# Four of twelve tiles get their router logits from VectorE, and their routing a step later

## The chip, the core and the metric

The kernel runs on one core of one Trainium2 chip. Its engines work side by side, each through its own queue in order: TensorE (matrix products), VectorE, ScalarE, GpSimd and SyncE (which here only issues DMAs). The time is the device time of one execution in microseconds; lower is better. The profiler's names are PE for TensorE, PEld for its weight loads, DVE for VectorE, ACT for ScalarE, POOL for GpSimd and SP for SyncE.

## What is computed

An attention with local and global keys, then a gated feed-forward block, then a layer of eight experts with one expert per token and a skip score. The change touches the seam between the last two:

```python
x = (silu * val) @ w_out                    # 1536 tokens x 512, end of the second block
skip_score = x @ w_skip                     # moe2: router
do_compute = skip_score > 0
logits = x[do_compute] @ w_gate             # 512 x 8
e_idx = argmax(logits); probs = softmax(logits)
y[e_idx == e] = gate * (relu(x @ w1[e]) @ w2[e])
out = x; out[do_compute] = x + y
```

## The kernel before

All of it is one program whose order is written out by hand; each engine works through its own list in that order and waits on semaphores where another engine's result is missing.

The second matrix product of the feed-forward block (`gemm2`) makes x for 12 tiles of 128 tokens, one tile in each step of `for t in range(11)`, and tile 11 behind the loop. A step is 36 products of 128x512 into one PSUM buffer: 12 blocks k of three products (h and w_out are split into a high and a low part). Three hooks, called behind blocks 1, 5 and 9, put the other work of the step between the products, so it stands in TensorE's queue at those places.

- At a step's start: `ranks(t-2)` (two small matmuls that count the tokens ahead in each expert, into a PSUM buffer), `select(t-2)` and `gates(t-2)` on VectorE (eight small instructions, L707 to L693; they end in `sel` and `val`).
- Hook `one`: `turn(t-1)` transposes x of the tile before on TensorE (L580) and ScalarE copies it to `x2t` (L581); `split_h(t+1)` makes the high and low part of h for the next step on ScalarE and VectorE (six instructions each, L567 and L568).
- Hook `two`: `routed(t-1)`: the logits by four matmuls of TensorE against `w9t` (w_gate and w_skip, 9 columns; each shows as two records in the trace), `route` on VectorE (L653 to L674: maximum, mask `oh`, running count `cum`, negated maximum), and `exps` on ScalarE (L677). Then `split_next`: casts of experts' weights, the high part on ScalarE (L845) and the low part on VectorE (L854), and `load_next`, loads of such weights on SP's queue.
- The third hook: `slots(t-2)`, one matmul that reads `sel` and `val`.

The logits and the ranks take turns in two PSUM buffers of one tag (`ps1`). The experts' raw weights and their casts live in slots: eight of a pool `raw`, and the tiles of h that have been used up. Eight chunks of 128x1024 are loaded ahead of the stage and cast in steps 2 (three), 3 (two), 6 (two) and 7 (one); four more are loaded in step 7 and six in step 10. Behind the stage, the experts take the other chunks as slots come free.

Of the kernel before, what the change touches and what calls it, by code (L numbers as in the profile page):

```python
# [8 lines left out]
F32 = mybir.dt.float32  # L9
# [6 lines left out]
ALU = mybir.AluOpType  # L16
# [11 lines left out]
def f(ap):  # L28
    return ap.bitcast(F32)
# [529 lines left out]
def split_h(s, t):  # L559
    nc = s.nc  # L560
    hh = s.hspool.tile([128, 12, 128], F32R, name="hh", bufs=2)
    hl = s.hspool.tile([128, 12, 128], F32R, name="hl", bufs=2)
    c = slice(128 * (t % 4), 128 * (t % 4) + 128)
    for q in range(6):
        i = slice(2 * q, 2 * q + 2)
        src = s.h[t // 4, q][:, :, c]
        nc.scalar.copy(hh[:, i, :], src)  # L567
        nc.vector.tensor_tensor(hl[:, i, :], src, f(hh[:, i, :]), ALU.subtract)  # L568
    s.hs[t] = hh, hl


def turn(s, t, h=None):

    nc = s.nc
    ks = range(4) if h is None else range(2 * h, 2 * h + 2)
    if not h:
        s.xt[t] = s.hpool.tile([128, 4, 128], F32, name="x2t", bufs=2)
    p = s.ps_n.tile([128, len(ks), 128], F32, name="pxt", tag="rb", bufs=2)
    for k in ks:
        nc.tensor.transpose(p[:, k - ks[0], :], s.x2[t][:, 128 * k:128 * k + 128], s.ident)  # L580
    nc.scalar.copy(s.xt[t][:, ks[0]:ks[-1] + 1, :], p)  # L581
# [7 lines left out]
        s.nc.tensor.matmul(s.lg[t], lhsT=s.xt[t][:, k, :], rhs=s.w9t[:, k, :], start=k == 0, stop=k == 3)  # L589


def gemm2(s, t, hooks={}):

    nc = s.nc
    hh, hl = s.hs.pop(t)
    x2 = s.x2[t] = s.hpool.tile([128, 512], F32, name="x2", bufs=3)

    N = 256 if t == 11 else 512
    for c in range(0, 512, N):
        p = s.ps_g.tile([128, N], F32, name="px", tag="ps0", bufs=2)  # L600
        n = 0
        for k in range(12):
            for h, w in ((hh, s.woh), (hh, s.wol), (hl, s.woh)):
                nc.tensor.matmul(p, lhsT=h[:, k, :], rhs=w[k][:, c:c + N], start=n == 0, stop=n == 35)  # L604
                n += 1
            if (c, k) in hooks:
                hooks[c, k]()
        nc.scalar.activation(x2[:, c:c + N], p, AF.Copy, scale=s.r[t // 6][:, t % 6:t % 6 + 1])
    nc.sync.dma_start(s.xm[128 * t:128 * t + 128, :], x2)
    if t < 11:  # L610
        nc.scalar.dma_start(s.out[128 * t:128 * t + 128, :], x2)
# [36 lines left out]
def route(s, t):  # L648

    V, p = s.nc.vector, s.ixpool if t == 11 else s.hpool  # L650
    lg, skip = s.lg[t][:, 0:8], s.lg[t][:, 8:9]
    m = s.rm[t] = (s.ixpool if t >= 10 else p).tile([128, 1], F32, name="rm", bufs=2)
    V.tensor_reduce(m, lg, AX.X, ALU.max)  # L653
    do = s.do = p.tile([128, 1], F32, name="rdo", bufs=2)
    V.tensor_scalar(do, skip, 0.0, None, ALU.is_gt)
    yield
    c = p.tile([128, 8], F32, name="rc", bufs=2)
    V.scalar_tensor_tensor(out=c, in0=lg, scalar=m, in1=s.m8, op0=ALU.is_equal, op1=ALU.mult)
    yield
    e = p.tile([128, 1], F32, name="re", bufs=2)  # L660
    V.tensor_reduce(e, c, AX.X, ALU.min)
    yield
    V.scalar_tensor_tensor(out=s.oh[:, t, :], in0=c, scalar=e, in1=do.to_broadcast([128, 8]),
                           op0=ALU.is_equal, op1=ALU.mult)
    yield
    V.tensor_scalar(s.val[:, t, 0, :], s.oh[:, t, :], s.tok1[:, t:t + 1], None, ALU.mult)
    V.tensor_tensor(s.cum[:, t + 1, :], s.cum[:, t, :], s.oh[:, t, :], ALU.add)


def exps(s, t):  # L670

    nc, V, p = s.nc, s.nc.vector, s.ixpool if t >= 10 else s.hpool
    m = s.rm[t]
    V.tensor_scalar(m, m, -1.0, None, ALU.mult)  # L674
    z = s.rz[t] = p.tile([128, 1], F32, name="rz", bufs=2)
    ex = p.tile([128, 8], F32, name="rex", bufs=2)
    nc.scalar.activation(ex, s.lg.pop(t)[:, 0:8], AF.Exp, bias=m, accum_out=z)  # L677


def gates(s, t):  # L680

    nc, V, p = s.nc, s.nc.vector, s.ixpool if t >= 10 else s.hpool
    z = s.rz.pop(t)
    V.tensor_scalar(z, z, 1e-9, None, ALU.add)
    yield
    V.reciprocal(z, z)
    yield
    g = p.tile([128, 8], F32, name="rg", bufs=2)
    V.tensor_scalar(g, s.oh[:, t, :], z, None, ALU.mult)
    yield  # L690
    V.tensor_copy(s.val[:, t, 1, :], g)
    yield
    V.tensor_tensor(s.val[:, t, 2, :], g, f(s.val[:, t, 1, :]), ALU.subtract)  # L693


def ranks(s, t, pool=None, tag="ps1"):

    rk = s.rk[t] = (pool or s.ps_g).tile([128, 8], F32, name="rk", tag=tag, bufs=1 if pool else 2)
    s.nc.tensor.matmul(rk, lhsT=s.ones16, rhs=s.cum[:, t, :], start=True, stop=False)
    s.nc.tensor.matmul(rk, lhsT=s.tri, rhs=s.oh[:, t, :], start=False, stop=True)  # L700


def select(s, t):

    V = s.nc.vector
    c = (s.ixpool if t >= 9 else s.hpool).tile([128, 8], F32, name="rp", bufs=2)
    V.tensor_tensor(c, s.oh[:, t, :], s.rk[t], ALU.mult)  # L707
    yield
    V.tensor_reduce(s.pos[:, t:t + 1], c, AX.X, ALU.add)
    yield  # L710
    sel = s.sel[t] = (s.ixpool if t >= 9 else s.hpool).tile([128, 256], F32R, name="sel", bufs=3 if t >= 9 else 2)
    V.tensor_scalar(sel, s.slot, s.pos[:, t:t + 1], None, ALU.is_equal)
    yield


def slots(s, t):

    if t in (0, 9):
        s.sl = s.ps_m.tile([24, 256], F32, name="sl", tag="misc", bufs=1)
    s.nc.tensor.matmul(s.sl, lhsT=s.val[:, t, :, :].rearrange("p a e -> p (a e)"), rhs=s.sel[t],  # L720
                       start=t in (0, 9), stop=t in (8, 11))


def run(*parts):

    parts = list(parts)
    while parts:
        parts = [p for p in parts if next(p, FAR) is None]
# [213 lines left out]
def attn_moe_kernel(ctx, tc, qx, kx, vx, rel, ints, wgv, w_out, rms_g, w9, w9t, w1, w2, out):  # L942
    s = K()
    nc = s.nc = tc.nc
# [4 lines left out]
    def pool(stack, name, side=None, space=None):  # L949
        kw = {} if space is None else {"space": space}  # L950
        return stack.enter_context(
            tc.tile_pool(name=name, bufs=1, side=side, reuse_waits="tile", **kw))
# [165 lines left out]
    rawpool = pool(phase3, "raw", side="right")  # L1118
# [11 lines left out]
        halves += [(j + 1, 0)] * (j < 8) + [(j, 1)]  # L1130
    loads = iter([(j, 4 * half + c) for j, half in halves for c in range(4)])
    s.slots = Slots()
    s.slots.add(rawpool, [f"raw{z}" for z in range(8)])

    def load_next(n, eng=nc.sync):
        for _ in range(n):
            x = next(loads, None)
            if x:
                if x == (8, 0):
                    experts[8].e = nc.values_load(  # L1140
                        s.eji[0:1, 0:1], engines=[mybir.EngineType.SP], min_val=0, max_val=7,
                        skip_runtime_bounds_check_because="a minimum with 7 of a count")
                experts[x[0]].load(x[1], eng)
# [5 lines left out]
    def split_next(n):  # L1149
        for _ in range(n):  # L1150
            x = next(chunks, None)
            if x:
                experts[x[0]].split(x[1], nc.scalar, nc.vector)

    load_next(8)
    s.early = s.ixpool.tile([128, 512], F32, name="early", bufs=1)
    nc.gpsimd.memset(s.early, 0.0)

    def routed(t):
        logits(s, t)  # L1160
        run(route(s, t))
        exps(s, t)

    for t in range(11):
        if t >= 2:
            ranks(s, t - 2)
            run(select(s, t - 2))
        if t >= 2:
            run(gates(s, t - 2))

        def one():
            if t >= 1:
                turn(s, t - 1)
                split_h(s, t + 1)
            if t in (2, 6, 10):
                for q in range(6):
                    s.slots.add(early if t < 10 and q == 0 else big, [f"h{t // 4}{q}"])
                load_next({6: 0, 10: 6}.get(t, 0))

        def two():  # L1180
            if t >= 1:
                routed(t - 1)
            split_next({2: 3, 3: 2, 6: 2, 7: 1}.get(t, 0))
            load_next({7: 4}.get(t, 0))

        gemm2(s, t, {(0, 1): one, (0, 5): two, (0, 9): lambda: t >= 2 and slots(s, t - 2)})


    slt = s.ixpool.tile([24, 256], F32, name="slt", bufs=1)
# [46 lines left out]
    def keep(n):  # L1236

        w = experts[0].w[0][0]
        for _ in range(n):
# [19 lines left out]
                                   op0=ALU.is_equal, op1=ALU.mult)  # L1259
# [82 lines left out]
    with tc.For_i(1, more, 1) as j:  # L1342
        lgi, lsi, lgate = job_slots(s, s.epool, ds(j, 1))
        e = nc.values_load(s.eji[0:1, ds(j, 1)], engines=[mybir.EngineType.SP], min_val=0, max_val=7,
                           skip_runtime_bounds_check_because="a minimum with 7 of a count")
# [85 lines left out]
```

## Time and profile before

| | before |
|---|---|
| median of three runs | 554.51 us (551.69 to 555.45) |
| the profiled execution | 554.08 us, its span 552.3 us |
| TensorE busy | 524.2 us (95%) |
| VectorE busy | 404.8 us (73%) |
| ScalarE busy | 277.5 us (50%) |
| GpSimd busy | 140.8 us (25%) |
| second matrix product, twelve steps | from 303.28 to about 428 us of the span |

The span is the profiled execution from its first to its last instruction. A timeline row gives the start, the length, the engine, the line and the instruction (output <- inputs, shapes); rows that follow each other on an engine may be joined with a count. The length of a row may overlap the next one on the same engine, so the distance of two starts is what a row takes of its queue. A row of busy time by stretch gives the stretch, its length, the busy us and the instructions (x) of TensorE, its weight loads, VectorE, ScalarE and GpSimd, then TensorE's granted clock as a share of full speed, the busy share of the DMA engines and GB/s. In the rows of waits, the engine in front waited for the one behind the arrow.

### The profile page before, as it was taken

The page shows a single profiled execution, that of the slowest core. Times are in us where ns is not written, and L with a number is a line of the kernel's source. Part 1 is how long each engine was busy: PE and PEld are TensorE (multiplying, and loading weights), DVE is VectorE, ACT ScalarE, POOL GpSimd, SP SyncE. Part 2 cuts the span into 40 slices and gives each one's busy share as a digit, 9 for nine tenths or more (in the row PEclk, how much of TensorE's full clock was granted, in tenths as well). Part 3 has the DMA queues.
Part 4 walks back from the last instruction along what each step waited for, and adds up shares of the span by engine and source line. Part 5 has one row for each costly group of instructions (what it writes and reads, how often), then busy time and mean ns, then how long its engine had stood idle before and what let it go on. Part 6 is the DMA issues. An engine that isn't in the chain of part 4 may idle for free. (4 is left out here: it accounts for less than half of the span.)

```text
span 552.3 us, 9096 instructions
## 1 busy us (share of the span) xinstructions
PE 524.2 (95%) x3132; PEld 425.8 (77%) x3132; DVE 404.8 (73%) x1026; ACT 277.5 (50%) x631; POOL 140.8 (25%) x140
## 2 busy tenths in 40 slices
PE   3899886999999999999999999999999999999994
PEld 2676665878888888888888888878789787888883
DVE  5899999567888688868884358456443599999971
ACT  2799896324332233333333255244231587988850
POOL 2446545001222212212220200000000512666001
PEclk9999998999999999999999999999999999999998
DMA  8653511112323323323313512116171599999300
GB/s 301 210 211 139 173 36 39 33 46 77 105 88 113 113 79 114 114 79 113 115 38 130 214 39 78 39 52 215 39 293 57 202 393 395 398 399 396 131 15 16
DMA packets 28997, 80.62 MB, mean 146 GB/s; under 512 B 3512, under 2 KB 3768, under 8 KB 28945
## 3 DMA queue, kind: packets, MB, share of 16 engines
q1 hardware_dynamic: 24400, 68.61, 35.0%
q0 software_dynamic: 2672, 8.22, 3.9%
q10 hardware_dynamic: 1872, 3.15, 1.6%
q8 instruction: 26, 0.43, 0.3%
q14 instruction: 27, 0.21, 0.1%
HBM read 72.28 MB, written 8.65 MB: 147 GB/s over the span
## 5 line engine op out<-in xcount | busy, mean ns | idle before, releaser
L538 PE MATMUL ps<-xh,wh 128*128 128x512 f32 (+1 forms) x304 | 115.4, 380 | 0.1
L538 PE MATMUL ps<-xh,wl 128*128 128x512 f32 (+1 forms) x304 | 115.0, 378 | 0.5 <-POOL wl L504 0.5
L538 PE MATMUL ps<-xl,wh 128*128 128x512 f32 (+1 forms) x304 | 114.9, 378 | 0.0
L854 DVE TENSOR_TENSOR ewl<-eraw,ewh 128x1024 fp32r<-128x1024 f32 x72 | 83.5, 1220 | 6.2 <-ACT ewh L845 5.9
L845 ACT CAST ewh<-eraw 128x1024 fp32r<-128x1024 f32 x72 | 71.3, 1055 | 6.2 <-DVE ewl L854 4.2
L538 PEld LDWEIGHTS ps<-xh,wl 128*128 128x128 f32 x304 | 57.2, 188 | 11.6 <-POOL wl L504 0.9
L491 DVE SCALAR_TENSOR_TENSOR wraw<-f64t,wraw 128x512 f32<-128x512 f32 x36 | 44.7, 1241 | 28.8 <-ACT f64t L489 28.8
L538 PEld LDWEIGHTS ps<-xh,wh 128*128 128x128 f32 x304 | 57.2, 188 | 11.0 <-issue 0.7
L538 PEld LDWEIGHTS ps<-xl,wh 128*128 128x128 f32 x304 | 57.2, 188 | 10.6
L604 PE MATMUL px<-woh,hh 128*128 128x512 f32 (+1 forms) x156 | 61.8, 396 | 0.0
L604 PE MATMUL px<-woh,hl 128*128 128x512 f32 (+1 forms) x156 | 58.7, 376 | 0.0
L604 PE MATMUL px<-wol,hh 128*128 128x512 f32 (+1 forms) x156 | 58.2, 373 | 0.0
L504 POOL TENSOR_TENSOR wl<-f64t,wh 128x512 fp32r<-128x512 f32 x24 | 31.0, 1293 | 101.3 <-ACT wh L503 55.7
L503 ACT CAST wh<-f64t 128x512 fp32r<-128x512 f32 x24 | 14.9, 622 | 71.4 <-DVE f64t L501 68.1
L262 ACT ACTIVATE es<-es,m 128x192 f32<-128x192 f32 (+1 forms) x96 | 41.4, 434 | 11.5 <-DVE m L251 10.3
L278 POOL TENSOR_SCALAR es<-es,z 128x192 f32<-128x192 f32 x46 | 36.0, 791 | 36.2 <-ACT pts L297 11.7
L286 PE MATMUL pt<-ident,es 128*128 128x128 f32 x176 | 30.5, 305 | 10.1 <-DVE pts L295 6.6
L286 PEld LDWEIGHTS pt<-ident,es 128*128 128x128 f32 x176 | 20.7, 152 | 21.6 <-DVE pts L295 10.0
L568 DVE TENSOR_TENSOR hl<-h,hh 128x256 fp32r<-128x256 f32 x72 | 25.4, 422 | 15.8 <-ACT hh L567 15.8
L604 PEld LDWEIGHTS px<-woh,hl 128*128 128x128 f32 x156 | 29.3, 188 | 5.8
L604 PEld LDWEIGHTS px<-woh,hh 128*128 128x128 f32 x156 | 29.4, 188 | 4.9
L604 PEld LDWEIGHTS px<-wol,hh 128*128 128x128 f32 x156 | 29.5, 189 | 4.0
(195 smaller groups left out, 979.7 us busy)
## 6 DMA issues: line engine op xcount, KB each, us to landing
eraw<-in_w_dram SPq DMA_DIRECT2D x64, 512.0 KB, 11.2
wraw<-in_wgv_dram SPq DMA_DIRECT2D x24, 512.0 KB, 3.8
wraw<-in_w_out_dram SPq DMA_DIRECT2D x12, 512.0 KB, 3.5
vp<-in_vx_dram SPq DMA_DIRECT2D x8, 704.0 KB, 4.0
eraw<-in_w_dram POOLq DMA_DIRECT2D x8, 512.0 KB, 13.6
kd<-in_kx_dram SPq DMA_DIRECT2D x7, 464.0 KB
xm<-x SPq DMA_DIRECT2D x12, 256.0 KB
out_dram<-x ACTq DMA_DIRECT2D x12, 256.0 KB, 2.8
```

The costliest lines, as they stand in the source:

```text
L262: nc.scalar.activation(e[:, r, x, e0:e0 + n], e[:, r, x, e0:e0 + n], AF.Exp, bias=m[:, j:j + 1], scale=-1.0, accum_out=z[:, j:j + 1])
L278: eng.tensor_scalar(e[:, r, x, e0:e0 + n], e[:, r, x, e0:e0 + n], z[:, j:j + 1], None, ALU.mult)
L286: nc.tensor.transpose(pt[:, kt, x, :], e[:, r, x, 128 * kt:128 * kt + 128], s.ident)
L491: nc.vector.scalar_tensor_tensor(out=a.bitcast(F32), in0=t, scalar=F64_LEAST, in1=a.bitcast(F32), op0=ALU.is_ge, op1=ALU.mult)
L503: nc.scalar.copy(hi, t)
L504: eng.tensor_tensor(lo, t, f(hi), ALU.subtract)
L538: nc.tensor.matmul(p, lhsT=w[:, k, :], rhs=x[c][:, k, a:b], start=n == 0, stop=n == 11)
L568: nc.vector.tensor_tensor(hl[:, i, :], src, f(hh[:, i, :]), ALU.subtract)
L604: nc.tensor.matmul(p, lhsT=h[:, k, :], rhs=w[k][:, c:c + N], start=n == 0, stop=n == 35)
L845: eng.copy(wh, raw)
L854: eng.tensor_tensor(wl, raw, f(wh), ALU.subtract)
```

## The change

Tiles 1, 3, 5 and 7 (`rows`) no longer get transposes and logits matmuls. `row_logits` takes their logits on VectorE: nine instructions, one for each column of w9, that multiply x of the tile (128x512) by a row of w9 which lies on all 128 partitions and sum the result into one number per token. Five of them stand in the first hook of the step behind the tile, four in the next step's. The routing of such a tile (`route`, `exps`) moves from the second hook of step t+1 to that of step t+2, ahead of the next tile's; its ranks, select and gates (`ranked`) move from the start of step t+2 to its third hook; its slots matmul moves from the third hook of step t+2 to the first hook of step t+3. The other tiles keep their places.

The nine rows of w9 are broadcast by five DMAs on SP's queue into five tiles `w9b`, in the place of five of the eight `raw` slots, which become slots again in step 9. Three chunks instead of eight are loaded ahead of the stage. Casts come two in step 2, one each in 3, 6, 7 and 8, and two in 9; loads come two in step 2, one each in 3, 6, 7 and 8, three in 9 and six in 10.

```diff
--- before.py
+++ after.py
@@ -589,6 +589,16 @@
         s.nc.tensor.matmul(s.lg[t], lhsT=s.xt[t][:, k, :], rhs=s.w9t[:, k, :], start=k == 0, stop=k == 3)
+def row_logits(s, t, es):
+    if es[0] == 0:
+        s.lg[t] = s.hpool.tile([128, 9], F32, name="lgd", bufs=1)
+    for e in es:
+        s.nc.vector.tensor_tensor_reduce(
+            out=s.w9b[4][:, 512:1024], in0=s.x2[t], in1=s.w9b[e // 2][:, 512 * (e % 2):512 * (e % 2) + 512],
+            scale=1.0, scalar=0.0, op0=ALU.mult, op1=ALU.add, accum_out=s.lg[t][:, e:e + 1])
 def gemm2(s, t, hooks={}):
     nc = s.nc
@@ -1130,7 +1140,11 @@
         halves += [(j + 1, 0)] * (j < 8) + [(j, 1)]
     loads = iter([(j, 4 * half + c) for j, half in halves for c in range(4)])
     s.slots = Slots()
-    s.slots.add(rawpool, [f"raw{z}" for z in range(8)])
+    s.slots.add(rawpool, [f"raw{z}" for z in range(3)])
+    s.w9b = [rawpool.tile([128, 1024], F32, name=f"w9b{z}", bufs=1) for z in range(5)]
+    for z in range(5):
+        rows = w9[2 * z:min(2 * z + 2, 9), :].rearrange("(o e) n -> o (e n)", o=1)
+        nc.sync.dma_start(s.w9b[z][:, 0:rows.shape[1]], rows.to_broadcast([128, rows.shape[1]]))
     def load_next(n, eng=nc.sync):
         for _ in range(n):
@@ -1152,7 +1166,7 @@
             if x:
                 experts[x[0]].split(x[1], nc.scalar, nc.vector)
-    load_next(8)
+    load_next(3)
     s.early = s.ixpool.tile([128, 512], F32, name="early", bufs=1)
     nc.gpsimd.memset(s.early, 0.0)
@@ -1161,29 +1175,53 @@
         run(route(s, t))
         exps(s, t)
+    rows = (1, 3, 5, 7)
+    def ranked(t):
+        ranks(s, t)
+        run(select(s, t))
+        run(gates(s, t))
     for t in range(11):
-        if t >= 2:
-            ranks(s, t - 2)
-            run(select(s, t - 2))
-        if t >= 2:
-            run(gates(s, t - 2))
+        if t >= 2 and t - 2 not in rows:
+            ranked(t - 2)
         def one():
+            if t - 3 in rows:
+                slots(s, t - 3)
             if t >= 1:
-                turn(s, t - 1)
+                if t - 1 not in rows:
+                    turn(s, t - 1)
                 split_h(s, t + 1)
+            if t - 1 in rows:
+                row_logits(s, t - 1, range(5))
+            if t - 2 in rows:
+                row_logits(s, t - 2, range(5, 9))
             if t in (2, 6, 10):
                 for q in range(6):
                     s.slots.add(early if t < 10 and q == 0 else big, [f"h{t // 4}{q}"])
-                load_next({6: 0, 10: 6}.get(t, 0))
+            if t == 10:
+                load_next(6)
         def two():
-            if t >= 1:
+            if t - 2 in rows:
+                run(route(s, t - 2))
+                exps(s, t - 2)
+            if t >= 1 and t - 1 not in rows:
                 routed(t - 1)
-            split_next({2: 3, 3: 2, 6: 2, 7: 1}.get(t, 0))
-            load_next({7: 4}.get(t, 0))
-        gemm2(s, t, {(0, 1): one, (0, 5): two, (0, 9): lambda: t >= 2 and slots(s, t - 2)})
+            if t == 9:
+                s.slots.add(rawpool, [f"w9b{z}" for z in range(5)])
+            split_next({2: 2, 3: 1, 6: 1, 7: 1, 8: 1, 9: 2}.get(t, 0))
+            load_next({2: 2, 3: 1, 6: 1, 7: 1, 8: 1, 9: 3}.get(t, 0))
+        def three():
+            if t - 2 in rows:
+                ranked(t - 2)
+            elif t >= 2:
+                slots(s, t - 2)
+        gemm2(s, t, {(0, 1): one, (0, 5): two, (0, 9): three})
     slt = s.ixpool.tile([24, 256], F32, name="slt", bufs=1)
```

What stands in the queues, first on VectorE in the middle of step 3 (`hl` is h's low part for the next step, `x_3564` is tile 1's x, `lgd` its logits; the bare `ISA lgd` reads the sum out). Before:

```order
L568 TENSOR_TENSOR hl<-h_2039,hh 128x256 [waits Activation_49]
L653 TENSOR_REDUCE rm<-lg 128x1 [waits PE_49]
L655 TENSOR_SCALAR rdo<-lg 128x1
L658 SCALAR_TENSOR_TENSOR rc<-lg,rm,m_3485 128x8 [waits DVE_49]
L661 TENSOR_REDUCE re<-rc 128x1 [waits DVE_49]
L663 SCALAR_TENSOR_TENSOR oh<-rc,re,rdo 128x8 [waits DVE_49]
```

Now:

```order
L568 TENSOR_TENSOR hl<-h_2039,hh 128x256 [waits Activation_49]
L597 ISA w9b_3509,lgd<-x_3564,w9b_3507 128x512 [waits DVE_49]
L597 ISA lgd 128x1
L597 ISA w9b_3509,lgd<-x_3564,w9b_3508 128x512 [waits DMAHW5_49,DVE_49]
L597 ISA lgd 128x1
L597 ISA w9b_3509,lgd<-x_3564,w9b_3508 128x512 [waits DVE_49]
L597 ISA lgd 128x1
L597 ISA w9b_3509,lgd<-x_3564,w9b_3509 128x512 [waits DMAHW6_49,DVE_49]
L597 ISA lgd 128x1
L663 TENSOR_REDUCE rm<-lgd 128x1
L665 TENSOR_SCALAR rdo<-lgd 128x1 [waits DVE_49]
L668 SCALAR_TENSOR_TENSOR rc<-lgd,rm,m_3485 128x8 [waits DVE_49]
```

Between the split of h and the first routing now stand four products of the row tile; the first routing is the row tile's (`lgd`), and the routing of the even tile follows it.

Second, ScalarE in step 3, from the last part of h's split (`rex` is the exponential, `ewh` the high part of a weight cast, `x_` the copy of the step's x out of PSUM). Before:

```order
L567 CAST hh<-h_2039 128x256
L677 ACTIVATE rex,rz<-lg,rm 128x8 [waits DVE_49,PE_49]
L845 CAST ewh<-eraw 128x1024 [waits DMAHW5_49]
L845 CAST ewh<-eraw 128x1024
L608 ACTIVATE x_3770<-px,r_1376 128x512 [waits DMAHW3_49,DMAHW0_49,PE_49]
```

Now:

```order
L567 CAST hh<-h_2039 128x256
L687 ACTIVATE rex,rz<-lgd,rm 128x8 [waits DVE_49]
L687 ACTIVATE rex,rz<-lg,rm 128x8 [waits DVE_49,PE_49]
L855 CAST ewh<-eraw 128x1024 [waits DMAHW2_49]
L618 ACTIVATE x_3735<-px,r_1376 128x512 [waits DMAHW3_49,PE_49]
```

There are two exponentials in a row where one stood, and one cast where two stood.

Third, TensorE over the end of step 3 and the start of step 4. Before (from the last product of step 3):

```order
L604 MATMUL px<-woh_2023,hl 128x512
L699 LDWEIGHTS ones_3498
L699 MATMUL rk<-cum,ones_3498 128x8
L700 LDWEIGHTS tri
L700 MATMUL rk<-oh,tri 128x8 [waits DVE_49]
L604 MATMUL px<-woh_2018,hh 128x512 [waits Activation_49]
L604 MATMUL px<-wol_2024,hh 128x512
L604 MATMUL px<-woh_2018,hl 128x512
L604 MATMUL px<-woh_2018,hh 128x512
L604 MATMUL px<-wol_2024,hh 128x512
L604 MATMUL px<-woh_2018,hl 128x512
L580 MATMUL pxt<-ident,x_3770 128x128 [waits Activation_49]
```

Now:

```order
L614 MATMUL px<-woh_2023,hl 128x512
L709 LDWEIGHTS ones_3498
L709 MATMUL rk<-cum,ones_3498 128x8 [waits Activation_49]
L710 LDWEIGHTS tri
L710 MATMUL rk<-oh,tri 128x8 [waits DVE_49]
L614 MATMUL px<-woh_2018,hh 128x512
L614 MATMUL px<-wol_2024,hh 128x512
L614 MATMUL px<-woh_2018,hl 128x512
L614 MATMUL px<-woh_2018,hh 128x512
L614 MATMUL px<-wol_2024,hh 128x512
L614 MATMUL px<-woh_2018,hl 128x512
L730 MATMUL sl<-sel,val 24x256 [waits DVE_49]
```

The ranks at the step's start (tile 2's in both) now wait for ScalarE too, and behind six products the slots matmul of tile 1 stands where a transpose stood.

## Rows read from the trace of the kernel before

**Rows 1.** Busy time in stretches: step 6 from 360.71, last step, experts; counts in brackets.

```profile
360.71:370.61 9.90, 9.90 (x54) 8.04 (x54) 6.28 (x24) 5.36 (x12) 0.00 (x0) 1.00 0.15 55
...
410.20:428.00 17.80, 17.79 (x144) 16.54 (x144) 6.18 (x38) 3.64 (x10) 1.27 (x1) 1.00 0.36 132
...
464.00:500.00 36.00, 36.00 (x172) 29.44 (x171) 36.00 (x39) 32.76 (x41) 21.56 (x6) 1.00 1.04 399
```

**Rows 2.** Waits, steps 2 to 10: who waited for whom, us in total, times, longest.

```profile
DVE rp L707 <- PE rk L700: 19.2, 7, 3.2
```

**Rows 3.** TensorE's timeline, steps 5 and 6: start us, us, line, instruction.

```profile
350.81 0.47 PE L604 MATMUL px<-woh,hh 128*128 128x512 f32 x1
...
352.26 0.60 PE L580 MATMUL pxt<-ident,x 128*128 128x128 f32 x4
...
352.62 0.48 PE L604 MATMUL px<-woh,hh 128*128 128x512 f32 x1
...
352.93 0.40 PE L604 MATMUL px<-wol,hh 128*128 128x512 f32 x1
...
353.16 0.40 PE L604 MATMUL px<-woh,hl 128*128 128x512 f32 x1
...
355.48 0.96 PE L589 MATMUL lg<-w9t,x2t 128*128 128x9 f32 x8
...
356.29 0.47 PE L604 MATMUL px<-woh,hh 128*128 128x512 f32 x1
...
359.13 0.28 PE L720 MATMUL sl<-sel,val 128*24 128x256 f32 x1
...
360.71 0.47 PE L604 MATMUL px<-woh,hh 128*128 128x512 f32 x1
```

**Rows 4.** VectorE's timeline, step 6 (from 360.71).

```profile
363.74 2.10 DVE L568 TENSOR_TENSOR hl<-h,hh 128x256 fp32r<-128x256 f32 x6 [1.15 <-ACT hh L567]
...
366.38 0.17 DVE L653 TENSOR_REDUCE rm<-lg 128x1 f32<-128x8 f32 x1 [0.53 <-PE lg L589]
...
367.04 0.23 DVE L663 SCALAR_TENSOR_TENSOR oh<-rc,re,rdo 128x8 bf16<-128x8 f32 x1
...
367.51 0.15 DVE L674 TENSOR_SCALAR rm<-rm 128x1 f32<-128x1 f32 x1
...
369.09 2.36 DVE L854 TENSOR_TENSOR ewl<-eraw,ewh 128x1024 fp32r<-128x1024 f32 x2 [1.43 <-ACT ewh L845]
...
371.36 0.16 DVE L707 TENSOR_TENSOR rp<-oh,rk 128x8 f32<-128x8 bf16 x1
...
372.87 0.17 DVE L693 TENSOR_TENSOR val<-rg,val 128x8 fp32r<-128x8 f32 x1
```

**Rows 5.** ScalarE's timeline, step 6.

```profile
367.75 0.27 ACT L677 ACTIVATE rex<-lg,rm 128x8 f32<-128x8 f32 x1 [2.51 <-DVE rm L674]
...
368.01 1.99 ACT L845 CAST ewh<-eraw 128x1024 fp32r<-128x1024 f32 x2
```

**Rows 6.** VectorE's instructions by shape: attention's add-and-reduce; busy us, mean ns.

```profile
L251 DVE CUSTOM_DVE_ANT_0 es<-sc,bias 128x192 f32<-128x192 f32 x80 | 25.3, 351 | 1.1 <-PE sc L240 1.1
...
L251 DVE CUSTOM_DVE_ANT_0 es<-sc,bias 128x64 f32<-128x64 f32 x8 | 1.7, 218 | 0.0
```

**Rows 7.** Line 491: duration ns min/median/max; one of its instructions in VectorE's timeline.

```profile
L491 DVE SCALAR_TENSOR_TENSOR wraw<-f64t,wraw x36: 678/1375/1798, 55.4 to 284.1; 128x512 f32<-128x512 f32 x36
...
185.00 0.69 DVE L491 SCALAR_TENSOR_TENSOR wraw<-f64t,wraw 128x512 f32<-128x512 f32 x1 [1.42 <-ACT f64t L489]
```

**Rows 8.** SP's timeline: the experts' loads after the stage.

```profile
432.65 74.05 SPq L837 DMA_DIRECT2D eraw<-in_w_dram  x46
```

**Rows 9.** Busy time in stretches, end of the attention: TensorE and its granted clock.

```profile
88.00:90.00 2.00, 0.40 (x8) 0.16 (x3) 2.00 (x9) 1.30 (x7) 2.00 (x3) 1.00 0.69 256
...
92.00:93.00 1.00, 1.00 (x12) 0.78 (x8) 0.93 (x4) 0.77 (x3) 0.58 (x2) 0.51 0.08 16
...
99.00:100.00 1.00, 1.00 (x8) 0.72 (x5) 0.00 (x0) 0.75 (x2) 0.00 (x0) 1.00 0.00 0
```

## Prediction

> **What bounds the kernel now.** I read the busy time by stretch first, the waits second, and then laid the rows of one step of the second matrix product side by side. That stage runs from about 303 to 428 us of a span of 552.3 us, in twelve steps, one tile of 128 tokens each. A full step takes 9.9 us and TensorE is busy in all of it, while VectorE and ScalarE are busy for five to six of it [rows 1]. In the list of waits of steps 2 to 10 no row has TensorE waiting for an engine: VectorE and ScalarE wait, among them VectorE for the ranks matmul, up to 3.2 us at a time [rows 2]. So a microsecond taken off TensorE's queue there is a microsecond off the time, as long as VectorE still delivers before TensorE comes to what it needs. After the stage, the experts' stage starts from what the stage leaves, and VectorE and the DMA engines are full there [rows 1]. Its loads wait for slots which the stage sets free (46 issues from 432.65 us on [rows 8]). I therefore let every gain or loss of the stage go through to the end unchanged.
>
> The question is thus what VectorE's and ScalarE's rows give to TensorE, and when. Time is counted below from S, the first product of an odd step (3, 5, 7 or 9). All four of them now carry the second part of a row tile, t-2, and the whole routing of two tiles.
>
> **What leaves TensorE.** For four tiles the four transposes and four logits matmuls go. The transposes hold the queue for 0.36 us (352.26 to 352.62) and lengthen the next product by 0.08 (0.31 to the one after, against 0.23). The logits hold it for 0.81 and again 0.08 [rows 3]. That is 1.33 us a tile, 5.3 us in all. Ranks and slots matmuls stay as many as before and only change place: 0 for their own durations. ScalarE loses four copies, which nothing waited for.
>
> **What a product costs on VectorE.** A multiply-and-sum over 128x512 is in no row. The same kind of instruction in the attention takes 218 ns for 64 columns and 351 ns for 192 [rows 6]: 1.04 ns per column, so 684 ns for 512. The listing shows that each waits for the one ahead of it (they share a scratch output). If they overlap like their neighbours the step from one to the next is 0.61 us, with the full wait it is 0.73. I take 0.69: four are 2.8 us, five are 3.5.
>
> [...] First the row: an instruction with two fp32 sources in SBUF and 512 columns (L491) takes between 678 and 1798 ns, with a median of 1375 [rows 7]. So the same form runs both at about 1.04 ns per column and at twice that. In the step of [rows 1] GpSimd is idle, as in its neighbours, and L491 takes 0.69 us at 185.00 [rows 7], where no GpSimd instruction lies beside it, so I count the product at the short end. [...]
>
> **An odd step, laid out.** VectorE's split of h ends at S+5.13 (363.74 plus 2.10, with S at 360.71) [rows 4]. Nothing before it changes: the even tile's transpose and copy stay. Four products bring VectorE to S+7.9. The row tile's routing follows: its mask oh is ready 0.89 us after the routing begins (366.38 to 367.04 plus 0.23), at S+8.8. TensorE comes to the ranks of that tile at the place where the slots matmul stood, at S+8.32 (350.81 to 359.13) [rows 3]. With 0.1 us for a handover between engines (VectorE's rm ended 0.09 us before the exponential began [rows 4, 5]) it waits 0.55 us.
>
> The second tile's routing starts 1.2 us after the first (the rows of one routing) at S+9.1. The exponential ends 1.64 us after a routing begins (366.38 to 367.75 plus 0.27 [rows 4, 5]), at S+10.75. The next ranks matmul writes the PSUM buffer that this exponential reads; before, logits and ranks never shared a buffer, now three of the four such places name ScalarE as releaser in the listing. TensorE would be there at S+9.87 plus 0.55, and waits about 0.45. So an odd step has 1.0 us of new waits, four make 4.0 us, and the even step begins at about S+10.9.
>
> **The even step behind it.** Its second hook puts the row tile's slots matmul after six products, 1.45 us into the step (350.81 to 352.26): TensorE is there at S+12.35. What it waits for stands on VectorE behind the odd step's weight casts. ScalarE's cast begins right after the exponential, 1.63 us after the second routing's start (366.38 to 368.01), at S+10.75; VectorE's half starts 1.08 later (369.09), and takes 1.18 (2.36 for two) [rows 4, 5]. Then come select and gates, 1.68 us from 371.36 to the end of 372.87. That is S+14.7, plus the handover: a wait of 2.4 us. Step 5 has no cast: select begins at S+10.4 and ends before S+12.3, so step 6 does not wait. Steps 3 and 7 have one cast, and steps 4 and 8 wait 2.4 us each. Step 9 has two casts, 1.18 more, and step 10 waits 3.6. Together 8.4 us. Before, select and gates also stood behind the casts, but the slots matmul that needs them came 8.3 us into the step and was never late; the cover was that distance, and it is gone. Behind the waiting slots matmul stands all of TensorE's queue.
>
> **The rest.** Over a pair of steps VectorE has 4.2 us of splits, 6.2 of products, 2.5 of routing, 3.4 of select and gates and up to 3.5 of casts, 19.8 at most, against 19.8 us for the pair before: so its queue never falls behind by more than a step, and the split for the next step, which TensorE needs at its start, stays early. On the SP queue five broadcasts of w9 take the place of five weight loads ahead of the stage, with no more bytes; the first product needs them in step 2, two steps later. The weight loads in steps 2, 3 and 6 to 9 stand two or more steps ahead of their casts, except those of steps 8 and 9, which feed the experts' stage: eighteen chunks are loaded and eight cast by its start, as before. I take 0 for these; if the nine late loads were not done in time, the first experts would wait, but their 4.7 MB take 12 us at the 399 GB/s of [rows 1], and the last step alone has 17.8.
>
> **Sum.** 4.0 + 8.4 - 5.3 = 7.1 us more. The profiled execution took 554.1 us by itself (span 552.3 us and 1.8 around it), against a median of 554.5. So 554.1 + 7.1 = **561.2 us**. With products 0.61 or 0.73 us apart and handovers between 0 and 0.2 us this case lies between 558.5 and 564.
>
> **Rivals.**
> *The waits do not come (faster).* VectorE is idle for a third or more of a step [rows 1], and if its rows came 2.4 us earlier than I laid them, every matmul would find its operands ready. The saving alone gives 554.1 - 5.3 = 548.8. It decides from select and gates ending by S+12.3 in cast steps. Against it: in the odd step nine rows of routing for two tiles, four products and the cast hang on each other in one queue. Chance 0.10.
> *The waits cancel the saving (same).* The short waits in odd steps vanish (products of 0.5 us, or handovers of nothing) and those at the slots shrink by 0.9 us each, to 1.5, 1.5 and 2.7: 5.7 - 5.3, about 554.5, and up to 559 on the way to my case. Chance 0.15.
> *Products at twice the length.* 0.69 us more for each: four in an odd step delay its ranks by 2.8 us, four times 11 us: 572. It needs the long form of [rows 7] without GpSimd. Chance 0.05.
> *The waits lower TensorE's clock.* Before, the granted clock stood at 1.00 in this stage [rows 1], where TensorE never paused. [...] Against it: around each wait the products stand close. Chance 0.15. [...]
>
> **How the numbers follow.** My forecast has 0.55. About 1% (5.5 us) is what a measurement of this kernel can tell from no change. Faster than 548.6 needs the first rival: 0.10. Slower than 559.6 are most of my case (0.45 of 0.55), the clock and the long products: 0.65. The rest is 0.25. From 556 to 571 all is held but the first rival, half of the second and the third, about 0.2.
>
> **What would show it.** In the changed profile, waits of TensorE for VectorE at slots in steps 4, 8 and 10 of some 2.4, 2.4 and 3.6 us and none in 6, and short ones at ranks in odd steps; steps of about 10.9, 11.0, 10.9, 8.5, 10.9, 11.0, 10.9 and 13.5 us from 3 to 10; products of 0.6 to 0.73 us. It is wrong if TensorE has no wait there, if the products take 0.4 or 1.3 us, if the clock falls, or if the experts' stage gets longer or shorter by itself.

## The result, and the profile after

The changed kernel takes 562.45 us (median of four runs, 561.57 to 563.54), the kernel before beside it 553.1 us (551.66 to 555.45). The ratio is 1.0148, with a 95% interval from 1.0127 to 1.0169: slower by about 8.2 us. The four runs of the kernel before lie in two pairs, near 551.7 and near 555 us, with its median between them, so the medians are 9.35 us apart where the ratio says 8.2. The forecast was 561.2 us.

| profiled execution | before | after |
|---|---|---|
| time | 554.08 us | 563.54 us, the longest of its four |
| span | 552.3 us | 561.8 us |
| second matrix product, first to last product's start | 119.50 us | 128.37 us |
| up to that stage | 303.28 us | 303.72 us |
| behind it | 129.5 us | 129.7 us |

So 8.87 of the 9.5 us arise in the stage. Its steps, each from its first product to the next step's first:

| step | 2 | 3 | 4 | 5 | 6 | 7 | 8 | 9 | 10 |
|---|---|---|---|---|---|---|---|---|---|
| before | 9.91 | 9.91 | 9.89 | 9.90 | 9.91 | 9.91 | 9.90 | 9.90 | 9.91 |
| forecast | - | 10.9 | 11.0 | 10.9 | 8.5 | 10.9 | 11.0 | 10.9 | 13.5 |
| after | 8.41 | 10.84 | 12.46 | 10.39 | 8.59 | 10.79 | 10.84 | 10.77 | 14.99 |

Where [rows 2] had no wait of TensorE in these steps, there are ten now. The list of waits of the changed kernel from 320 to 430 us (us in total, times, longest):

```profile
PE sl L730 <- DVE val L703: 7.5, 3, 3.2
PE rk L710 <- DVE oh L673: 1.4, 4, 0.4
PE rk L709 <- ACT rex L687: 1.1, 3, 0.4
```

TensorE's timeline shows them one by one. At 338.65 and 340.68 are the two of step 3, then the slots matmuls of steps 4, 6, 8 and 10; that of step 6 has no wait:

```profile
338.65 0.17 PE L710 MATMUL rk<-oh,tri 128*128 128x8 bf16 x1 [0.39 <-DVE oh L673]
...
340.68 0.17 PE L709 MATMUL rk<-cum,ones 128*128 128x8 bf16 x1 [0.39 <-ACT rex L687]
...
344.47 0.30 PE L730 MATMUL sl<-sel,val 128*24 128x256 f32 x1 [2.11 <-DVE val L703]
...
365.06 0.29 PE L730 MATMUL sl<-sel,val 128*24 128x256 f32 x1
...
386.70 0.30 PE L730 MATMUL sl<-sel,val 128*24 128x256 f32 x1 [2.11 <-DVE val L703]
...
409.45 0.30 PE L730 MATMUL sl<-sel,val 128*24 128x256 f32 x1 [3.24 <-DVE val L703]
```

What VectorE did ahead of step 3's wait for the mask and step 4's for `val`, in step 3 (from 329.89) and the start of step 4; rows between are left out:

```profile
332.88 2.11 DVE L568 TENSOR_TENSOR hl<-h,hh 128x256 fp32r<-128x256 f32 x6 [1.69 <-ACT hh L567]
334.90 0.69 DVE L597 CUSTOM_DVE_ANT_0 w9b<-x,w9b 128x512 f32<-128x512 f32 x1
335.51 0.09 DVE L597 DVE_READ_ACCUMULATOR2_ANT lgd<- 128x1 f32 x1
335.63 0.69 DVE L597 CUSTOM_DVE_ANT_0 w9b<-x,w9b 128x512 f32<-128x512 f32 x1
...
337.72 0.16 DVE L663 TENSOR_REDUCE rm<-lgd 128x1 f32<-128x8 f32 x1
...
338.37 0.23 DVE L673 SCALAR_TENSOR_TENSOR oh<-rc,re,rdo 128x8 bf16<-128x8 f32 x1
...
341.60 1.23 DVE L864 TENSOR_TENSOR ewl<-eraw,ewh 128x1024 fp32r<-128x1024 f32 x1 [1.42 <-ACT ewh L855]
342.75 0.15 DVE L717 TENSOR_TENSOR rp<-oh,rk 128x8 f32<-128x8 bf16 x1
...
344.25 0.17 DVE L703 TENSOR_TENSOR val<-rg,val 128x8 fp32r<-128x8 f32 x1
```

The mask `oh` is done at 338.60, and the ranks matmul runs at 338.65. Select (342.75) begins only when the cast has ended, `val` is done at 344.42, and the slots matmul runs at 344.47: a handover of 0.05 us each time.

The waits are 10.0 us, and the steps 2 to 10 grew by 98.08 - 89.14 = 8.94 us, though TensorE also gave work away. The granted clock tells what else came in. Busy time by stretch (columns as in [rows 1]), steps 4, 6, 8 and 10:

```profile
340.73:353.19 12.46, 10.35 (x40) 7.97 (x40) 9.41 (x33) 3.36 (x8) 0.00 (x0) 0.86 0.26 85
...
363.58:372.17 8.59, 8.59 (x41) 6.83 (x40) 8.07 (x32) 3.98 (x10) 0.00 (x0) 1.00 0.36 123
...
382.96:393.80 10.84, 8.73 (x40) 6.82 (x40) 9.42 (x34) 4.31 (x9) 0.00 (x0) 1.00 0.12 48
...
404.57:419.56 14.99, 11.75 (x54) 9.25 (x54) 8.41 (x32) 5.14 (x12) 0.00 (x0) 0.89 0.76 255
```

Closer, behind the slots matmuls of steps 4, 8 and 10:

```profile
346.00:347.00 1.00, 1.00 (x4) 0.81 (x3) 1.00 (x5) 0.00 (x0) 0.00 (x0) 0.50 0.90 354
...
386.70:388.00 1.30, 1.30 (x7) 1.08 (x8) 1.12 (x7) 1.00 (x2) 0.00 (x0) 1.00 0.00 0
...
410.00:411.00 1.00, 1.00 (x5) 0.81 (x4) 0.85 (x6) 0.65 (x2) 0.00 (x0) 0.50 1.04 402
```

In steps 4 and 10 the granted clock fell to 0.50 after TensorE had resumed; in step 8, behind a wait of the same 2.11 us, it stayed at 1.00. At the low level a product takes 0.42 us of the queue instead of 0.23 (two neighbours in step 4, and in step 8):

```profile
345.50 0.63 PE L614 MATMUL px<-woh,hh 128*128 128x512 f32 x1
345.92 0.63 PE L614 MATMUL px<-wol,hh 128*128 128x512 f32 x1
```

```profile
387.53 0.39 PE L614 MATMUL px<-woh,hh 128*128 128x512 f32 x1
387.76 0.40 PE L614 MATMUL px<-wol,hh 128*128 128x512 f32 x1
```

With step 6 as the even step without a wait, the 8.94 us come apart. The waits are +10.0. The row tiles save 1.50 in step 2 and 1.32 in each of 4, 6 and 8: -5.5. The clock costs 1.6 in step 4 (12.46 - 8.59 - 2.11 - 0.14) and 1.7 in step 10 (14.99 - 9.91 - 3.24 - 0.14): +3.3. The 0.14 is what step 8 is longer beside its listed wait (10.84 - 8.59 - 2.11); three of them, and 0.15 beside the listed waits in each odd step, are +1.0. Sum: 8.8. The 0.15 is not the price of a wait: step 5 of the run with two outputs below has no wait in its list, has the ranks in their new place, and takes 10.03 us, 0.13 more than before.

Behind the stage little changed; the last step and the experts' stretch, which answer to the second and third row of [rows 1]:

```profile
419.56:437.30 17.74, 17.73 (x144) 16.48 (x144) 6.17 (x38) 3.63 (x10) 1.27 (x1) 1.00 0.33 121
...
472.00:508.00 36.00, 36.00 (x175) 29.34 (x174) 36.00 (x39) 31.88 (x40) 20.70 (x6) 1.00 1.04 398
```

### The profile page after: what moved, and what is told of

Read it like the earlier page. It is cut to its first block, busy times and chain, and to the rows that moved or that the text cites. A ratio compares the mean times of both kernels' runs of the same rounds, so it can differ in the third digit from the quotient of the medians.

```text
span 561.8 us, 9084 instructions
## 1 busy us (share of the span) xinstructions
PE 522.9 (93%) x3084; PEld 423.1 (75%) x3084; DVE 428.2 (76%) x1098; ACT 275.6 (49%) x627; POOL 140.3 (25%) x140
```

## Experiments

Each edit is against the changed kernel. Ratios are to the kernel before, which ran on the same chip (medians 554.45 to 554.81 us); "stage" is the first to the last product's start, 119.50 us before and 128.37 after.

### Casts, loads and broadcasts alone

```diff
-    rows = (1, 3, 5, 7)
+    rows = ()
```

> The set of row tiles is empty: all twelve tiles take their logits from TensorE as before, but the five broadcasts of w9 and the new places of casts and loads stay. This takes the moved casts and loads by themselves. Theory (as in the prediction, which counted them at nothing): no difference from the kernel before, within 1 us of it, steps of 9.9 us and no wait of TensorE in the stage. Rival: the broadcasts or the shifted loads cost part of the 9.5 us by which the span of the changed kernel is longer, so 1 to 3 us more than before, seen as a later start of the stage (303.7 instead of 303.3 us), or as an experts' stage that is longer than before.

Measured: 554.66 us, ratio 0.9998 (0.9982 to 1.0013). No step is longer than 9.92 us, there is no wait of TensorE in the stage, and the stage has 119.50 us. It begins at 303.76 us though; in the other runs it begins anywhere from 303.26 to 304.68, in no relation to their edits, so half a microsecond ahead of the stage can't be put down to the change. Moved casts, loads and broadcasts cost nothing by themselves.

### One row tile, at two places

```diff
-    rows = (1, 3, 5, 7)
+    rows = (3,)
```

> Only tile 3 takes its logits from VectorE. Its odd step is step 5, which has no cast, and step 6 is the one whose slots matmul did not wait. Theory (price by place): step 4 is 1.3 us shorter, step 5 about 0.5 longer (the wait for the mask and its restart), step 6 as before: 0.9 us less than before in all, about 1 us under it. Rival (every row tile costs the same share of the 9 us): 2.3 us more than before.

Measured: 553.98 us, ratio 0.9986 (0.9968 to 1.0004). Step 4 has 8.43 us, step 5 has 10.39 with one wait of 0.33, step 6 has 10.03: 28.85 us for the three against 29.70 before, 0.85 less where 0.9 was expected. The stage has 118.24. Its other steps are some 0.05 us shorter each, as are the untouched steps of the next run; no run shows why. The interval of the time includes no change.

```diff
-    rows = (1, 3, 5, 7)
+    rows = (7,)
```

> Only tile 7 takes its logits from VectorE. Its odd step is step 9, with two casts, and its slots matmul stands in step 10, where TensorE waited 3.24 us. Theory (price by place): step 8 is 1.3 us shorter, step 9 about 0.9 longer, step 10 longer by the wait of 3.2 and, if the clock falls behind it as it did, by 1.7 more: 4.6 us more than before, or 3.0 if the clock stays. Rival (every row tile costs the same share): 2.3 us more.

Measured: 558.3 us, ratio 1.0062 (1.0047 to 1.0077), some 3.4 us more. Its waits in TensorE's timeline:

```profile
398.68 0.17 PE L710 MATMUL rk<-oh,tri 128*128 128x8 bf16 x1 [0.33 <-DVE oh L673]
...
400.72 0.17 PE L709 MATMUL rk<-cum,ones 128*128 128x8 bf16 x1 [0.38 <-ACT rex L687]
...
405.64 0.41 PE L730 MATMUL sl<-sel,val 128*24 128x256 f32 x1 [3.24 <-DVE val L703]
```

Steps 8, 9 and 10 have 8.44, 10.78 and 15.02 us, the last with a stretch at half clock. The time lies between the two that were expected, 3.0 us more if the clock stays up and 4.6 if it falls. Its two longest executions (559.76 and 560.13 us, the last the profiled one) have a mean granted clock of 0.985, the three shortest (557.25 to 558.17 us) one of 0.991 or 0.992, so the clock probably did not fall there in every execution.

The same move of work is a small gain in its own steps for tile 3, as expected, and a loss for tile 7. The tiles differ in what stands between the routing and the slots matmul; the runs with moved casts and slots below test that. An equal share of 2.3 us is outside both intervals.

### The waits filled with work

```diff
             if t - 3 in rows:
+                fill({4: 9, 8: 9, 10: 14}.get(t, 0), t)
                 slots(s, t - 3)
```

`fill(n, t)` issues n products of 128x512 into a PSUM tile that nothing reads.

> The changed kernel with idle products of 128x512 into an unused PSUM tile ahead of the slots matmul of a row tile: 9 in steps 4 and 8, 14 in step 10, none in step 6 (2.0 and 3.2 us at 0.227 us each). TensorE waits as long for the same thing, but works while it does. Theory (the pause is what lowers the clock): no stretch at 0.50 in steps 4 and 10, these steps 1.6 and 1.7 us shorter, the time about 3.3 us under the changed kernel's, 559. Rival (the clock falls for another reason, such as the instructions that run then): the same stretches at 0.50 and 562.5.

Measured: 560.65 us, ratio 1.0106 (1.0091 to 1.0120), some 2 us under the changed kernel where 3.3 were expected. Steps 4, 8 and 10 have 10.87, 10.84 and 13.42 us instead of 12.46, 10.84 and 14.99; the stage has 125.23. Stretches behind the slots matmuls of steps 4 and 10:

```profile
344.00:350.00 6.00, 5.97 (x28) 4.86 (x29) 5.69 (x21) 0.06 (x1) 0.00 (x0) 1.00 0.36 107
...
407.00:413.00 6.00, 5.92 (x33) 4.85 (x32) 4.98 (x24) 2.42 (x7) 0.00 (x0) 1.00 0.98 329
```

Nothing but the pause was taken away, and the clock stayed up in both steps. For step 10 this shows that the pause makes it fall, since the clock fell there in every profile that has the pause. For step 4 it shows less: in a second profile of the changed kernel, below, the clock stayed up there with the pause too, so one of the two falls of the first profile is not in every execution, which fits the smaller gain. Step 8, which had not lost its clock, did not change. In the profiles of this document a gap of 3.2 us was followed by the lower clock in four of four cases, one of 2.1 us in one of six.

### The slots matmul later

```diff
         def one():
-            if t - 3 in rows:
-                slots(s, t - 3)
...
         def three():
+            if t - 3 in rows:
+                slots(s, t - 3)
             if t - 2 in rows:
```

> The changed kernel with one move: a row tile's slots matmul goes from the first hook of step t+3 to its third, ahead of the other slots matmul there; casts, routing and ranks keep their places. Theory (the lost distance is the cause): VectorE's last value is there 3.6 to 4.8 us into steps 4, 8 and 10, TensorE now comes 8 us in, so the waits of 2.11, 2.11 and 3.24 us, the 0.14 us lost at each restart and the stretches at half clock (1.6 us in steps 4 and 10) all go: 11 us, to 551.4; steps 4 and 8 of 8.6 us, step 10 of 10.0, odd steps still 10.4 to 10.9. Rival (VectorE's queue is full and TensorE only meets it elsewhere): a pair of steps is now 19.4 us, and VectorE's rows of a pair with two casts are close to it; the splits of h come late and 1 to 2 us a pair are lost again: 554 to 557, with waits of TensorE for the split.

Measured: 553.71 us, ratio 0.9988 (0.9970 to 1.0005). Steps 4, 6 and 8 have 8.53, 8.54 and 8.53 us, steps 9 and 10 have 11.21 and 10.99: the slots waits are gone, with their clock. The stage has 118.52, some 9.9 us less, and not 11: the waits of the odd steps stay, step 9's for the mask grows to 0.76, and step 10 has a new one, for ScalarE's copy of x out of PSUM:

```profile
397.09 0.17 PE L710 MATMUL rk<-oh,tri 128*128 128x8 bf16 x1 [0.76 <-DVE oh L673]
...
401.60 0.66 PE L580 MATMUL pxt<-ident,x 128*128 128x128 f32 x4 [0.80 <-ACT x L618]
```

That copy stands on ScalarE behind the two casts of step 9. So TensorE does meet a late engine elsewhere, as the rival has it, but in steps 9 and 10 alone, and in step 10 it is ScalarE and not VectorE's split of h.

### The casts behind select and gates

```diff
         def three():
             if t - 2 in rows:
                 ranked(t - 2)
+                casts()
```

`casts` is the `split_next` and `load_next` of the second hook, which steps without such a tile keep there.

> The changed kernel with the weight casts and loads of odd steps moved from the second hook to behind select and gates of the row tile in the third; the slots matmul stays in the first hook of the next step. Theory (the casts between routing and select make the slots late): select can begin when the second routing ends, 1.2 us or more before TensorE reaches the next step, and ends 0.4 us before TensorE comes to the slots matmul, in steps 4, 8 and 10 alike: those waits fall to 0.3 us or less, the clock stays up, 551.5. Rival (the cast is only part of it, select is late by itself): a wait of about 1 us stays in each of these steps, with two restarts at half clock, 556 to 558.

Measured: 552.42 us, ratio 0.9971 (0.9955 to 0.9987). The slots matmul stands where the change put it, and does not wait; the whole list of the stage is

```profile
PE rk L710 <- DVE oh L673: 1.4, 4, 0.4
PE pxt L580 <- ACT x L618: 1.0, 1, 1.0
```

So the slots waits need both: the casts ahead of select, and the slots matmul near. Take either away and they are gone. The ranks' wait for the exponential went too; no run shows why.

### Ranks and slots later

```diff
         def one():
             if t - 3 in rows:
-                slots(s, t - 3)
+                ranked(t - 3)
...
         def three():
-            if t - 2 in rows:
-                ranked(t - 2)
-            elif t >= 2:
+            if t - 3 in rows:
+                slots(s, t - 3)
+            if t >= 2 and t - 2 not in rows:
                 slots(s, t - 2)
```

> The changed kernel with two moves: the row tile's ranks, select and gates go from the third hook of its odd step to the first hook of the even step behind it (where the slots matmul stood), and its slots matmul to the third hook there. Theory: the mask is ready 0.4 us after TensorE's old place for the ranks and 2 us ahead of the new one, and the ranks no longer take the PSUM buffer that the exponential reads at the old distance, so all ten waits go and the saving of 1.33 to 1.5 us for each row tile is left: 5.5 us under the kernel before, 548.6 to 549, ratio 0.990; odd steps of 9.9 us, even ones of 8.5, step 10 of 9.9. Rival (VectorE bounds the pair): select and gates of two tiles, the casts and the five products now all stand in the even step on VectorE, the split for the next step comes late, TensorE waits 1 to 2 us a pair: 551 to 555.

Measured: 552.71 us, ratio 0.9974 (0.9955 to 0.9993): 1.4 us under before, not 5.5. Steps 3 to 8 are as expected (9.98, 8.70, 9.91, 8.67, 9.91, 8.68), but steps 9 and 10 have 11.08 and 11.87:

```profile
395.97 0.17 PE L709 MATMUL rk<-cum,ones 128*128 128x8 bf16 x1 [0.49 <-DVE cum L677]
...
396.83 0.17 PE L710 MATMUL rk<-oh,tri 128*128 128x8 bf16 x1 [0.69 <-DVE oh L673]
...
400.15 0.66 PE L580 MATMUL pxt<-ident,x 128*128 128x128 f32 x4 [1.64 <-ACT x L618]
```

Here the rival held: with casts in steps 7 and 8 too, VectorE came late into step 9 (its split of h from 389.88, close behind a cast), and ScalarE's copy of x came behind the two casts of step 9 (397.53 to 399.51). That the casts are the reason is read from their order here, and tested in the last run of the section on all waits below.

### Two outputs for the products

```diff
-            out=s.w9b[4][:, 512:1024], in0=s.x2[t], ...
+            out=s.early if e % 2 else s.w9b[4][:, 512:1024], in0=s.x2[t], ...
```

The memset of `early` moves to step 10.

> The changed kernel with the unread output of the products going to two tiles in turn (the second is a tile that the kernel only needs at the end; its memset moves to step 10), so a product waits for the one two ahead of it, not for the last. Theory (the wait on the engine's own result sets the distance of 0.735 us): products 0.61 us apart as the attention's are, four are 0.5 us sooner, the masks are there when TensorE comes (four waits of 0.35 and their restarts gone), the exponential too: odd steps of 9.9 to 10.2 us, up to 3.5 us less; but TensorE is then earlier at the slots, whose waits grow by some 0.4 us each: 559.5 to 561. Rival (the distance is the length of the product plus the reading of the sum): 0.73 us as before and 562.5.

Measured: 562.1 us, ratio 1.0144 (1.0117 to 1.0172), not to be told from 1.0148. The distance of the products:

```profile
325.15 0.69 DVE L597 CUSTOM_DVE_ANT_0 w9b<-x,w9b 128x512 f32<-128x512 f32 x1
...
325.76 0.69 DVE L597 CUSTOM_DVE_ANT_0 early<-x,w9b 128x512 f32<-128x512 f32 x1
...
326.38 0.69 DVE L597 CUSTOM_DVE_ANT_0 w9b<-x,w9b 128x512 f32<-128x512 f32 x1
```

0.61 us now, against 0.73 in the changed kernel (334.90 to 335.63): the wait on the engine's last result costs 0.12 us each time. The four waits for the mask are gone, and the odd steps have 10.48, 10.03, 10.42 and 10.42 us, 1.4 us less in all. The slots waits stay at 2.1, 2.1 and 3.2 and the exponential's at 0.4: VectorE's and ScalarE's rows came as much sooner as TensorE did. The time hides the 1.4 us: the runs lie at 560.4 us (two, mean granted clock 0.987) and at 562.1 to 562.9 (three, 0.980). The profiled one, at 560.4, lost its clock in step 10 alone and has a stage of 125.36 us; the changed kernel with one such fall has 126.82, below.

### All waits out

The edits of the two sections before together, and step 9's second cast to step 10:

```diff
-            split_next({2: 2, 3: 1, 6: 1, 7: 1, 8: 1, 9: 2}.get(t, 0))
-            load_next({2: 2, 3: 1, 6: 1, 7: 1, 8: 1, 9: 3}.get(t, 0))
+            split_next({2: 2, 3: 1, 6: 1, 7: 1, 8: 1, 9: 1, 10: 1}.get(t, 0))
+            load_next({2: 2, 3: 1, 6: 1, 7: 1, 8: 1, 9: 3, 10: 1}.get(t, 0))
```

> The moves of the run with late ranks and slots and the two output tiles together, and one of the two casts of step 9 moved to step 10 (with one of step 10's loads behind it), because in the runs with late slots two casts on ScalarE in step 9 held its copy of x out of PSUM, for which TensorE waited 0.8 to 1.6 us in step 10. Theory: no wait of TensorE over 0.1 us is left in steps 3 to 10, odd steps of 9.9 us, even ones of 8.5, step 10 of 9.9; stage 114 us against 119.5, 5.5 us less than before: 548.6 to 549, ratio 0.990. Rival (VectorE's queue lags in some pair once TensorE is faster: a pair of steps would be 18.4 us): waits of 0.2 to 0.7 us for masks or for the split of h come back, 551, ratio 0.994 to 0.996.

Measured: 550.13 us, ratio 0.9910 (0.9896 to 0.9925), between the theory and the rival. Two waits are left:

```profile
PE pxt L580 <- ACT x L618: 0.7, 1, 0.7
PE rk L710 <- DVE oh L673: 0.4, 1, 0.4
```

Then all casts of steps 8 and 9 went to step 10:

```diff
-            split_next({2: 2, 3: 1, 6: 1, 7: 1, 8: 1, 9: 1, 10: 1}.get(t, 0))
-            load_next({2: 2, 3: 1, 6: 1, 7: 1, 8: 1, 9: 3, 10: 1}.get(t, 0))
+            split_next({2: 2, 3: 1, 6: 1, 7: 1, 10: 3}.get(t, 0))
+            load_next({2: 2, 3: 1, 6: 1, 7: 1, 8: 1, 9: 3, 10: 3}.get(t, 0))
```

> The kernel of the run with all waits out, with the casts of steps 8 and 9 moved to step 10 too, which has no products of a row tile (three casts there, three of its six loads behind them). Theory (the casts of steps 8 and 9 made VectorE late for the mask, 0.40 us, and ScalarE late with its copy of x, 0.68): both waits and their restarts go, step 9 of 9.6 and step 10 of 9.7 us instead of 10.1 and 10.9: 1.7 us less, a stage of 112.9 us, about 548.4, ratio 0.988. Rival (what is moved comes due later): three casts in step 10 and the later loads hold back the first expert, whose stage starts 0.5 to 1.5 us later behind tile 11: 549.5 to 550.1, no gain over the run before.

Measured: 548.88 us, ratio 0.9891 (0.9874 to 0.9907): 6 us faster than before. No wait of TensorE is left from 320 us to the start of the experts; from there on to 440 us the one row is

```profile
PE eph L904 <- ACT exh L894: 0.4, 1, 0.4
```

which the kernel before has too. A pair of steps (7 and 8: 9.61 and 8.67) is 18.28 us against 19.81; the stage has 113.20, and the first expert starts at 423.80 us instead of 428.72, although this run's stage began 1.4 us later.

### The changed kernel once more

> The changed kernel unaltered, for a second profile of it. Theory (waits are fixed by the order, the clock behind them is not): the same ten waits within 0.1 us each, but the stretches at half clock may stand behind other waits or be missing: a stage of 125.2 us with none, 126.8 with one, 128.4 with two, 130 with three. Rival (the fall of the clock belongs to steps 4 and 10 and to what runs there): again steps 4 and 10 and not step 8, 128.4.

Measured: 561.97 us, one execution. The same ten waits, 7.5, 1.4 and 1.1 us in all, but step 4 has 10.83 us now and step 10 has 15.08; the stage has 126.82, as expected for one fall. The two stretches:

```profile
344.00:350.00 6.00, 5.47 (x25) 4.56 (x26) 5.65 (x22) 0.55 (x2) 0.00 (x0) 1.00 0.43 129
...
407.00:413.00 6.00, 5.13 (x20) 4.28 (x20) 4.19 (x18) 2.42 (x7) 0.00 (x0) 0.72 0.92 324
```

So the wait of 2.1 us in step 4 brings the low clock in one execution and not in the next. The wait of 3.2 us in step 10 brought it in all four profiles that have that pause (this, the first, the two-output run and tile 7 alone), the waits of 2.1 us in one of six. What decides is open.

## Why the prediction held, step by step

- **TensorE's queue sets the stage, and the stage the end.** Right: 8.87 us in the stage, 9.5 in the span, and the runs that took waits away got them back at the end.
- **Saving of 1.33 us a row tile.** Right: 1.32 in step 6, and 1.4 to 1.5 in steps whose ranks went elsewhere as well (step 2, and those of tiles 3 and 7 alone). The new places of ranks and slots, put at 0, were not free: 0.13 us in an odd step without a listed wait.
- **The product.** Forecast 0.69 us apart, between 0.61 and 0.73; measured 0.73, and 0.61 once the wait on the own result was gone. Both bounds were exact and the choice was wrong: the listing had shown that each waits for the last, so the upper one applied. Without it the mask's four waits are gone. The length is 684 to 694 ns for all 36, the short end of [rows 7]; none takes the 1375 ns that are the median there.
- **Odd steps.** Forecast 0.55 and 0.45 us, 4.0 in all; measured 0.33 to 0.39 and 0.37 to 0.39, the latter three times, 2.5 in all, and 0.6 in places that no wait shows. The three places for the exponential were in the prediction's own words; the sum counted four.
- **Even steps.** Forecast 2.4, 0, 2.4 and 3.6 us; measured 2.11, 0, 2.11 and 3.24. The mechanism is shown from both sides (casts moved, slots moved). With S at 329.89, `val` came at S+14.53 instead of S+14.7, and TensorE at S+12.5 instead of S+12.35.
- **The clock.** Given 0.15 as a case of its own. It did come, twice in the first profile and once in the second, at 1.6 to 1.7 us each: the low level of 0.50, like the 0.51 of [rows 9], lasts some 3.4 us behind the pause (345.1 to 348.5). The waits came out 2.4 us smaller than forecast and the clock, left out of the likeliest case, gave 1.6 to 3.3 back. That the time agreed to 1.3 us is in part luck: two errors of opposite sign, the clock one of them.
- **Casts, loads, broadcasts at nothing.** Right (ratio 0.9998). "VectorE never falls behind by more than a step" held for the changed kernel. It was cover lent by TensorE's own waits: without them VectorE and ScalarE were late in steps 9 and 10, by up to 1.6 us.

## What to carry to other kernels

Work taken off the bounding engine pays only if what it still has to read from the slower path is as far ahead as before; when a result is made a step later, move its consumers a step later too, and look at what stands ahead of it in the new producer's queue. Here the move was worth -6 us with the consumers late, the casts out of the way and two outputs for the products, and +8 without. Try one tile first, at the quietest place and at the busiest: the steps behind the two pointed to the cause.

## What the hardware showed beside that

- A pause of TensorE of 2.1 us was followed by the lower clock in one of six cases, one of 3.2 us in four of four. In the five profiled falls the clock fell from 0.1 us before TensorE resumed (tile 7 alone: a granted clock of 0.76 from 404 to 407 us puts a fall from 1.00 to 0.50 at about 405.56, an estimate, and TensorE resumed at 405.64) to 1.3 us after it (two outputs: the first product that takes 0.39 us of the queue instead of 0.23 starts at 407.51, and TensorE had resumed at 406.25). It came back under steady products: in step 4 of the first profile the granted clock is 0.50 from 345.1 to 348.5 us and 1.00 from 348.5 to 349, with TensorE busy throughout.
- A wait on the engine's own last result costs VectorE 0.12 us for an instruction of 0.69 us (0.73 against 0.61 us from one to the next), since without it the next one starts 0.08 us before the last ends.
